# Last matrix product in seven products: row scaling on ScalarE, products without weight sums first, high and low splits ordered by when they are due

## The chip, the cores and the metric

One core of one Trainium2 chip runs the whole program. The metric is the device time of one execution in microseconds (us); smaller is better. The engines are named as in the profile: PE (TensorE matmuls; PEld its weight loads), DVE (VectorE), ACT (ScalarE), POOL (GpSimd) and SP (SyncE, which issues the transfers here).

## The reference, cut to what matters

```python
attn = softmax(mask(q @ k.T / 8)) @ v            # 2 x 12 heads, 448 x 64, causal
x    = attn as 896 x 768
g    = h * sigmoid(h),  h = x @ moe_w_in         # 768 -> 2048
x    = g @ moe_w_out                             # 2048 -> 768
h    = x @ moe2_w_in                             # 768 -> 1024
e    = exp(h - max(h));  sm = e / (sum(e) + 1e-9)
solu = h * sm
ln   = (solu - mean) / sqrt(var + 1e-6) * g_ln   # over the 1024 columns
out  = ln @ moe2_w_out                           # 1024 -> 768
```

The change concerns the last two products and what lies between: `moe2_w_in` (called GEMM3 here), the chain of softmax and normalization, and `moe2_w_out` (GEMM4, weights `w4`).

## The kernel before, in words

**Precision.** Every matrix product runs on operands split into a high and a low part, and each step of the inner dimension is three matmuls: high by high, high by low, low by high. The high part is a copy on ACT, the low part a subtraction on DVE or POOL. Names that end in `h` and `l` are these parts. Weights arrive as 64-bit floats in chunks of 128 rows by 384 columns; each chunk is put together by one ACT operation (L275) and three bit operations on DVE (L280, L296, L286).

**GEMM3 and the chain.** 896 rows are 7 tiles of 128, t = 0 to 6. `gemm3(t)` makes `h` of one tile in PSUM. `chain` then does for this tile: maximum (DVE L675), exp (ACT L676), reciprocal (DVE L678, L679), product with h (DVE L680), mean (L681), square (ACT L683, which writes over `h` in PSUM), centring (ACT L684), and the power -1/2 of the variance (DVE L685, POOL L686). The result of a tile is the row `e`; its factor `rstd` is applied at the output. Two PSUM places hold `h`, so a tile's GEMM3 waits for L683 of two tiles before.

**GEMM4's weights.** The 16 chunks of `w4` are named as quarters "11", "12", "21", "22" (half of the rows, half of the columns), four chunks of each, k = 0 to 3. `feed4` takes them in while GEMM3 runs: `scale4` multiplies a chunk by `g_ln` (POOL L588), `high4` and `low4` split quarters 11, 21 and 22 (ACT L593, DVE L599), and after the four chunks of one k `sums4` forms the sums t1 to t4 of quarters in place (POOL L606 to L609). An engine's work is issued in the order in which the code calls it.

**GEMM4's products.** Tile 0 is multiplied plainly (`alone(0)` and `alone(1)`). Tiles 1 to 6 go in three pairs, and a pair's 2 x 2 quarters are multiplied by seven products instead of eight (`pair4`): 11·11, 12·21 and s4·22 with quarters of the weights, and s2·t2, s3·t3, s1·t1 and 22·t4 with weight sums. s1 to s4 are sums of quarters of the pair's own operand. Each product is 12 matmuls of 384 columns into one PSUM bank; its result is scaled by `rstd` and added to others (ACT L795, L796, DVE L786) and stored. The operand's quarters are transposed on PE (`turned`, L702, four transposes to a quarter), the sums formed by `sums` (ACT L725 copies, DVE L695 adds), and `parts` splits each (high ACT L691, low DVE or POOL L692); `take` calls it. Low parts of s1 to s4 are POOL's. Transposed quarters lie in two PSUM buffers (`tp`), so a further quarter waits until an earlier one has been read.

**The order.** After GEMM3: the first quarters of pair 0, `split_t` of t2 (ACT L869, DVE L870), then `alone(0)`, `split_t` of t3, the chain of tile 6 with `split_t` of t1 and t4 called inside it, then the three pairs. Between a pair's products, `ahead(g)` turns, sums and splits the operand of the next pair, step n after the n-th product.

Of the kernel before, what the change touches and what calls it, by code (L numbers as in the profile page):

```python
# [26 lines left out]
K2 = KF2 // 2  # L27
# [53 lines left out]
def fused(ctx, tc, qk, vv, w1, w2, w3, w4, gl, out):  # L81
# [11 lines left out]
    wring = pool("wring", 4)  # L93

    ident = const.tile([128, 128], F32, name="ident")

    def pad(where, count):
        where.tile([128, count // 4], F32, name="pad", tag="pad", bufs=1)

    pad(act, 64)  # L100
    pad(gap, 192)
    xhl = act.tile([128, 2, KD, T], F32R, name="x", tag="a")
    xh, xl = xhl[:, 0], xhl[:, 1]
# [2 lines left out]
    with tc.manual_schedule():  # L106
# [361 lines left out]
        for f in range(KF):  # L468
            if f == 1:
                gps[f, 1] = gm.tile([128, 512], F32, name="ps", tag="gm")  # L470
            else:
                t = pair()
                for b in range(B):
                    if f >= 2 or b == 1:
                        gps[f, b] = t[b]
            for half in range(2):
                for b in range(B):
                    if f >= 2 or b == 1:
                        gemm1(f, half, b)
                m = 2 * f + half + 4  # L480
                feed_to(*((1, m) if m < N12 else (2, m - N12)))
            for b in range(B):
                if f >= 2 or b == 1:
                    silu(f, b)
        warm = const.tile([128, 1], F32, name="warm")
        nc.scalar.activation(warm, ident[:, :1], AF.Exp)
        sgr.release()
# [84 lines left out]
        aop = {z: [dp.tile([128, K2, 128], F32R, name=f"a{z}{q}", tag=f"a{z}{q}") for q in "hl"]  # L572
               for z in ("u1", "u2", "11")}
        usum = dp.tile([128, K2, 128], F32, name="us", tag="us")
        gain = dp.tile([128, KF2], F32, name="gain", tag="gain", bufs=1)
        nc.sync.dma_start(gain, gl)

        def quad(m):
            n, k = divmod(m, KF2)
# [4 lines left out]
        def scale4(m):  # L584
            z, k = quad(m)
            x = quads[z, k] = wx.pop((4, m))
            g = gain[:, m % KF2:m % KF2 + 1]
            nc.gpsimd.tensor_scalar(x, x, g, None, ALU.mult)  # L588

        def high4(m):  # L590
            z, k = quad(m)
# [16 lines left out]
            nc.gpsimd.tensor_tensor(b22, b22, b11, ALU.subtract)  # L608
            nc.gpsimd.tensor_tensor(b21, b21, b22, ALU.subtract)  # L609

        scaled = []

        def feed4():
            m = fed[0]
            fed[0] += 1
            while scaled:
                old = scaled.pop(0)
                high4(old)
                low4(old)
            for _ in range(2):  # L620
                if len(pend) > (_ > 0):
                    old = order[pend.pop(0)][1]
                    scale4(old)
                    scaled.append(old)
            if m < len(order):
                conv_b(*order[m], x4, order[m + 1] if m + 1 < len(order) else None)
                pend.append(m)
            if m + 1 < len(order):
                conv_a(*order[m + 1])
            if m + RAWS < len(order):  # L630
                load_w(*order[m + RAWS])

# [33 lines left out]
        def half(t, n):  # L666
            return row(t)[:, K2 * n:K2 * n + K2]

        def chain(t, fill, fill2):
            ps = hps[t]  # L670
            s = dp.tile([128, 12], F32, name="s", tag="s", bufs=NT)
            es4[t] = dp.tile([128, KF2, 128], F32, name="e", tag="e", bufs=NT - 1)
            e, p4 = row(t), ps.rearrange("p n (m q) -> p (n m) q", m=K2)
            col = lambda m: s[:, m:m + 1]
            nc.vector.tensor_reduce(col(0), ps, AX.XY, ALU.max, negate=True)  # L675
            nc.scalar.activation(e, p4, AF.Exp, bias=col(0), accum_out=col(1))  # L676
            fill()
            nc.vector.tensor_scalar(col(2), col(1), 1e-9, None, ALU.add)  # L678
            nc.vector.reciprocal(col(3), col(2))  # L679
            nc.vector.scalar_tensor_tensor(e, e, col(3), p4, ALU.mult, ALU.mult, accum_out=col(4))  # L680
            nc.vector.tensor_scalar(col(5), col(4), -1.0 / DF2, None, ALU.mult)  # L681
            fill2()
            nc.scalar.activation(p4, e, AF.Square, bias=col(5), accum_out=col(6))  # L683
            nc.scalar.activation(e, e, AF.Identity, bias=col(5))  # L684
            nc.vector.tensor_scalar(col(7), col(6), 1.0 / DF2, 1e-6, ALU.mult, ALU.add)  # L685
            nc.gpsimd.tensor_tensor(col(9), col(7), mhalf, ALU.pow)  # L686
            rstd[t] = col(9)

        def parts(z, x, low):
            h, l = aop[z]  # L690
# [90 lines left out]
        def pair4(g, between):  # L781
            a, b = 2 * g + 1, 2 * g + 2
            ra, rb = rstd[a], rstd[b]

            def scaled_sum(o, ps, r, more):
                nc.vector.scalar_tensor_tensor(o, ps, r, more, ALU.mult, ALU.add)  # L786

            def made(z, q):
                ps = bank()
                product(ps, z, q, True, True)  # L790
                return ps

            ps = made("11", "11")
            m1a, m1b = four()
            nc.scalar.activation(m1a, ps, AF.Copy, scale=ra)  # L795
            nc.scalar.activation(m1b, ps, AF.Copy, scale=rb)  # L796
            between(0)
            ps = made("s2", "t2")
            u2a, u2b = four()
            scaled_sum(u2a, ps, ra, m1a)  # L800
            scaled_sum(u2b, ps, rb, m1b)
            between(1)
            ps = made("12", "21")
            c11, c22 = four()
            scaled_sum(c11, ps, ra, m1a)
            store(a, 0, c11)
            between(2)
            ps = made("s3", "t3")
            u3, v = four()
            scaled_sum(u3, ps, rb, u2b)  # L810
            between(3)
            ps = made("s1", "t1")
            scaled_sum(c22, ps, rb, u3)
            store(b, 1, c22)
            scaled_sum(v, ps, ra, u2a)
            between(4)
            ps = made("22b" if g % 2 else "22", "t4")
            c21, c12 = four()
            scaled_sum(c21, ps, rb, u3)
            store(b, 0, c21)  # L820
            between(5)
            ps = made("s4", "22")
            scaled_sum(c12, ps, ra, v)
            store(a, 1, c12)
            between(6)

        def fill():
            if scaled or pend or fed[0] < len(order):
                feed4()

        for t in range(NT):
            gemm3(t, (lambda: turn(0, "11")) if t == NT - 1 else None)
            if t == 0:
                fill()
            if t == NT - 3:
                turn_alone()
            if t == NT - 2:
                turn(0, "21")
                turn(0, "22")

            def first():
                if t == NT - 3:
                    take_alone()
                if t == NT - 2:
                    sums(0, [1])
                fill()

            if t < NT - 1:
                chain(t, first, fill)
        while scaled or pend or fed[0] < len(order):  # L850
            fill()
        take(0, "11")
        sums(0, [2, 3])
        area = act.tile([128, 2 * KD * T], F32R, name="area", tag="a")[:, 8:]
        take(0, "s2")
        take(0, "22")
        turn(0, "12")
        take(0, "12")
# [2 lines left out]
        banks[1] = pool("psq", 2, space=PS)  # L861
        w3p.release()
        t4p = pool("t4", side="right")

        def split_t(z, q):
            split[4, z] = [t4p.tile([128, K2, CH], F32R, name=f"{z}{p}", tag=f"{z}{p}") for p in "hl"]
            h, l = split[4, z]
            for k in range(K2):
                nc.scalar.activation(h[:, k], quads[q, k], AF.Copy)  # L869
                nc.vector.tensor_tensor(l[:, k], quads[q, k], h[:, k].bitcast(F32), ALU.subtract)  # L870

        split_t("t2", "22")
        take(0, "s3")
        alone(0)
        split_t("t3", "12")
        take(0, "s1")
        take(0, "s4")

        def split_sum():
            take(0, "us")  # L880

        chain(NT - 1, lambda: split_t("t1", "11"), lambda: (split_t("t4", "21"), split_sum()))

        pad(t4p, 224)

        def ahead(g):
            def step(n):
                if g > 2:
                    return
                if n == 1:  # L890
                    turn(g, "21")
                    turn(g, "22")
                    sums(g, [1])
                    take(g, "22")
                if n == 2:
                    turn(g, "11")
                    take(g, "11")
                    sums(g, [2, 3])
                    take(g, "s2")
                if n == 3:  # L900
                    turn(g, "12")
                    take(g, "12")
                    sums(g, [4])
                    take(g, "s3")
                if n == 4:
                    take(g, "s1")
                if n == 6:
                    take(g, "s4")
            return step

        for g in range(3):
# [56 lines left out]
```

## Time and profile before

| | |
|---|---|
| median of 3 runs | 446.78 us (446.25 to 447.24) |
| profiled execution, own time | 446.85 us |
| its span in the trace | 445.1 us |
| mean granted TensorE clock | 0.979 |
| PE busy | 421.1 us (95%) |
| DVE busy | 351.2 us (79%) |
| POOL busy | 233.9 us (53%) |
| ACT busy | 230.6 us (52%) |
| chain that ended last, by engine | PE 80%, DVE 11%, ACT 4%, POOL 3% |

The span runs from the first to the last instruction of the trace; the profiled execution's own time is 1.75 us longer. GEMM3 ends and GEMM4 begins near 362 us; the last matmul starts near 440 us. Busy shares are means over stages with different limits, so the text below reads stretches, not means.

### The profile page before, as it was taken

What the parts mean: (1) busy time and instruction counts of PE and PEld (TensorE: products, weight loads), DVE (VectorE), ACT (ScalarE), POOL (GpSimd) and SP (SyncE); (2) the same over time, 40 slices, a digit from 0 to 9 for tenths busy, and PEclk for the clock granted to TensorE, in tenths of its full rate; (3) what the DMA queues carried; (4) which work ended last, traced back from release to release, by engine and by line L of the source; (5) the groups of instructions that cost most, each with busy time, mean ns of one, the idle gap of its engine ahead of it and who ended that gap; (6) DMA issues with size and microseconds to landing.
All of it is one profiled execution on the core that took longest, in us unless ns stands there. A gap on an engine that the chain in (4) does not pass through costs nothing.

```text
span 445.1 us, 7468 instructions
## 1 busy us (share of the span) xinstructions
PE 421.1 (95%) x2581; PEld 375.0 (84%) x2581; DVE 351.2 (79%) x744; ACT 230.6 (52%) x536; POOL 233.9 (53%) x245
## 2 busy tenths in 40 slices
PE   8999999999999999999999999999989975769995
PEld 6667777999999999999999999998868755769995
DVE  4999997999999989886958889577796877584631
ACT  5999997444343443444434444343663754752300
POOL 3996973676776757542534344244466277223300
PEclk9999999999999999999999999999999995969999
DMA  8941414243243333454747575241232100001112
GB/s 270 351 159 47 160 30 129 71 143 117 98 142 104 110 112 102 122 161 144 219 138 225 160 215 181 83 130 36 71 108 68 38 1 1 18 18 54 54 42 64
DMA packets 19798, 50.03 MB, mean 112 GB/s; under 512 B 2352, under 2 KB 4528, under 8 KB 19760
## 3 DMA queue, kind: packets, MB, share of 16 engines
q1 hardware_dynamic: 19760, 49.56, 35.3%
q8 instruction: 20, 0.33, 0.3%
q14 instruction: 18, 0.15, 0.1%
HBM read 46.80 MB, written 2.75 MB: 111 GB/s over the span
## 4 chain that ended last, share of the span: by engine, by line
PE 80%; DVE 11%; ACT 4%; POOL 3%; issue 1%; POOLq 0%; SPq 0%; ACTq 0%
PE h L371 8%; PE h L370 8%; PE h L372 8%; PE h L497 7%; PE h L496 7%; PE h L498 7%; PE x L248 5%; PE ps L756 4%; PE ps L758 4%; PE ps L757 4%; DVE e L188 3%; PE x L158 2%; PE x L222 2%; PE x L168 2%; ACT e L676 2%; DVE s L675 2%
## 5 line engine op out<-in xcount | busy, mean ns | idle before, releaser
L306 POOL TENSOR_TENSOR wl<-wx,wh 128x384 fp32r<-128x384 f32 x64 | 79.3, 1241 | 90.9 <-ACT wh L302 88.6
L286 DVE SCALAR_TENSOR_TENSOR wx<-wr,wx 128x384 uint32<-128x384 uint32 x96 | 69.9, 728 | 0.1
L275 ACT ACTIVATE wr<-wr 128x384 f32<-128x384 f32 x96 | 52.8, 555 | 32.7 <-DMA wr<-w_in 32.6
L302 ACT ACTIVATE wh<-wx 128x384 fp32r<-128x384 f32 x64 | 33.4, 522 | 65.5 <-DVE wx L286 33.6
L371 PE MATMUL h<-x,wh 128*128 128x448 f32 x174 | 63.2, 363 | 0.0
L370 PE MATMUL h<-x,wh 128*128 128x448 f32 x174 | 63.1, 362 | 0.0
L296 DVE TENSOR_SCALAR wr<-wr 128x384 uint32<-128x384 uint32 x96 | 60.4, 631 | 2.9 <-DMA wr<-w_in 2.8
L372 PE MATMUL h<-x,wl 128*128 128x448 f32 x174 | 62.6, 360 | 0.0
L280 DVE SCALAR_TENSOR_TENSOR wx<-wr 128x384 uint32<-128x384 uint32 x96 | 61.1, 636 | 1.3 <-POOL gl L380 1.3
L497 PE MATMUL h<-gl,wh 128*128 128x448 f32 x160 | 58.1, 363 | 0.0
L496 PE MATMUL h<-gh,wh 128*128 128x448 f32 x160 | 58.0, 362 | 0.0
L498 PE MATMUL h<-gh,wl 128*128 128x448 f32 x160 | 57.6, 360 | 0.0
L208 POOL TENSOR_TENSOR e<-e,st 128x384 f32<-128x384 f32 (+3 forms) x72 | 46.2, 677 | 14.1 <-ACT e L194 6.9
L380 POOL TENSOR_TENSOR gl<-sg,gh 128x448 fp32r<-128x448 f32 x32 | 41.0, 1281 | 15.3 <-DVE gh L379 14.6
L194 ACT ACTIVATE e<-e,st 128x128 f32<-128x128 f32 (+3 forms) x84 | 43.6, 523 | 4.3 <-DVE st L188 4.3
L188 DVE CUSTOM_DVE_ANT_0 e<-x,mask 128x384 f32<-128x384 f32 (+3 forms) x84 | 33.0, 443 | 4.7 <-PE x L158 4.7
L654 PE MATMUL h<-w3h,y 128*128 128x512 f32 x84 | 33.4, 397 | 2.0 <-ACT h L683 2.0
L370 PEld LDWEIGHTS h<-x,wh 128*128 128x128 f32 x174 | 32.7, 188 | 2.6
L372 PEld LDWEIGHTS h<-x,wl 128*128 128x128 f32 x174 | 32.5, 187 | 2.3
L371 PEld LDWEIGHTS h<-x,wh 128*128 128x128 f32 x174 | 32.7, 188 | 1.6
L656 PE MATMUL h<-w3h,y 128*128 128x512 f32 x84 | 32.9, 391 | 0.0
L655 PE MATMUL h<-w3l,y 128*128 128x512 f32 x84 | 32.8, 391 | 0.0
(184 smaller groups left out, 896.2 us busy)
## 6 DMA issues: line engine op xcount, KB each, us to landing
wr<-w_in SPq DMA_DIRECT2D x96, 384.0 KB, 3.6
qk<-qk_in SPq DMA_DIRECT2D x11, 480.0 KB, 5.3
v<-vv_in SPq DMA_DIRECT2D x12, 256.0 KB, 6.2
out<-o SPq DMA_DIRECT2D x12, 192.0 KB, 1.9
out<-ou SPq DMA_DIRECT2D x4, 96.0 KB, 2.2
qk<-qk_in SPq DMA_DIRECT2D x2, 128.0 KB, 2.3
qk<-qk_in SPq DMA_DIRECT2D x1, 224.0 KB, 2.6
gain<-gl_in SPq DMA_DIRECT2D x1, 4.0 KB, 1.5
```

What stands on the lines that cost most here:

```text
L188: nc.vector.tensor_tensor_reduce(o, scs[p, u[0], u[1]], m, -SCALE, 3.0e38, ALU.add, ALU.min, st[p % 4][:, COL[u]:COL[u] + 1])
L275: nc.scalar.activation(high, high, AF.Copy, scale=DOWN)
L280: nc.vector.scalar_tensor_tensor(x.bitcast(U32), r[:, :, 1], 0x80000000, r[:, :, 0], ALU.bitwise_and, ALU.bitwise_or)
L286: nc.vector.scalar_tensor_tensor(xu, r[:, :, 1], 3, xu, ALU.logical_shift_left, ALU.bitwise_or)
L296: nc.vector.tensor_scalar(low, low, 29, None, ALU.logical_shift_right)
L306: eng.tensor_tensor(l, wx.pop((n, c)), h.bitcast(F32), ALU.subtract)
L370: nc.tensor.matmul(ps[:, :S], wh, rh, start=turn == 0 and k % NB == 0, stop=False)
L371: nc.tensor.matmul(ps[:, :S], wh, rl, start=False, stop=False)
L372: nc.tensor.matmul(ps[:, :S], wl, rh, start=False, stop=turn == 1 and k % NB == NB - 1)
L496: nc.tensor.matmul(ps[:, :S], wh, rh, start=f == 0, stop=False)
L497: nc.tensor.matmul(ps[:, :S], wh, rl, start=False, stop=False)
L498: nc.tensor.matmul(ps[:, :S], wl, rh, start=False, stop=f == KF - 1)
```

## The change

1. `gain` (the vector `g_ln`) moves into a pool that lives from the start, and its transfer is issued earlier.
2. `scale4` becomes an ACT activation (copy with a scale per row) in place of POOL's `tensor_scalar`, 16 times.
3. `feed4` scales and splits off the high parts of up to two chunks at once, then puts together the next chunk, then calls `low4`, whose last act is `sums4`.
4. A pair's products come in the order 11·11, 12·21, s4·22, s2·t2, s3·t3, s1·t1, 22·t4; before it was 11·11, s2·t2, 12·21, s3·t3, s1·t1, 22·t4, s4·22. The output sums are regrouped to suit.
5. `chain` becomes a generator with three stops. The chain of tile 6 and `split_t` of t3, t1 and t4 move into pair 0, between its products (`begin`). t1's low parts go to POOL. The turning of the next pair comes one or two steps later.

```diff
+    gain = const.tile([128, KF2], F32, name="gain")
...
+        nc.sync.dma_start(gain, gl)
         warm = const.tile([128, 1], F32, name="warm")
...
-            g = gain[:, m % KF2:m % KF2 + 1]
-            nc.gpsimd.tensor_scalar(x, x, g, None, ALU.mult)
+            nc.scalar.activation(x, x, AF.Copy, scale=gain[:, m % KF2:m % KF2 + 1])
...
-            while scaled:
-                old = scaled.pop(0)
-                high4(old)
-                low4(old)
-            for _ in range(2):
-                if len(pend) > (_ > 0):
-                    old = order[pend.pop(0)][1]
-                    scale4(old)
-                    scaled.append(old)
+            old = [order[pend.pop(0)][1] for _ in range(min(2, len(pend) - (len(pend) > 2)))]
+            for c in old:
+                scale4(c)
+                high4(c)
             if m < len(order):
                 conv_b(*order[m], x4, order[m + 1] if m + 1 < len(order) else None)
                 pend.append(m)
             if m + 1 < len(order):
                 conv_a(*order[m + 1])
+            for c in old:
+                low4(c)
...
-            ps = made("s2", "t2")
-            u2a, u2b = four()
-            scaled_sum(u2a, ps, ra, m1a)
-            scaled_sum(u2b, ps, rb, m1b)
-            between(1)
             ps = made("12", "21")
             c11, c22 = four()
             scaled_sum(c11, ps, ra, m1a)
             store(a, 0, c11)
+            between(1)
+            ps = made("s4", "22")
+            m13, u3 = four()
+            scaled_sum(m13, ps, ra, m1a)
             between(2)
+            ps = made("s2", "t2")
+            u2a, u2b = four()
+            scaled_sum(u2a, ps, ra, m13)
+            scaled_sum(u2b, ps, rb, m1b)
+            between(3)
             ps = made("s3", "t3")
...
+        def split_t(z, low=None):
+            q = {"t1": "11", "t2": "22", "t3": "12", "t4": "21"}[z]
             h, l = split[4, z]
             for k in range(K2):
                 nc.scalar.activation(h[:, k], quads[q, k], AF.Copy)
+                (low or nc.vector).tensor_tensor(l[:, k], quads[q, k], h[:, k].bitcast(F32), ALU.subtract)
...
+        late = chain(NT - 1)
+        next(late)
+
+        def begin(n):
+            if n == 0:
+                split_t("t3")
+                take(0, "s3")
+            if n == 1:
+                next(late)
+                take(0, "s1")
+                split_t("t1", nc.gpsimd)
+            if n == 2:
+                split_t("t4")
+            if n == 3:
+                next(late)
+                take(0, "us")
 
         def ahead(g):
             def step(n):
+                if g == 1:
+                    begin(n)
                 if g > 2:
                     return
-                if n == 1:
+                if n == 2:
                     turn(g, "21")
                     turn(g, "22")
                     sums(g, [1])
                     take(g, "22")
-                if n == 2:
+                if n == 3:
                     turn(g, "11")
                     take(g, "11")
                     sums(g, [2, 3])
-                    take(g, "s2")
-                if n == 3:
+                if n == 4:
                     turn(g, "12")
                     take(g, "12")
                     sums(g, [4])
+                    take(g, "s4")
+                if n == 5:
+                    take(g, "s2")
                     take(g, "s3")
-                if n == 4:
+                if n == 6:
                     take(g, "s1")
```

How this changes the order on the engines, at the three places that matter below. Line numbers of the changed kernel differ a little: L587 is the scaling, L592 and L598 the high and low parts of the quarters, L677 and L678 the square and the centring, L686, L687 and L690 the operand's high parts, low parts and adds, L867 and L868 the high and low parts of the t's, L669, L672 to L675 and L679 the chain on DVE, L680 the power on POOL, L781 the scaled sums.

ACT at the end of GEMM3, before. `b11h`, `b21h`, `b22h` are high parts of quarters, `a11h` the high part of pair 0's first operand quarter:

```order
L593 ACTIVATE b22h<-wx 128x384
L275 ACTIVATE wr<-wr 128x384
L593 ACTIVATE b11h<-wx 128x384
L683 ACTIVATE h,s<-e,s 128x1024
L684 ACTIVATE e<-e,s 128x1024
L593 ACTIVATE b21h<-wx 128x384
L593 ACTIVATE b22h<-wx 128x384
L691 ACTIVATE a11h<-tp 128x512
```

The same place after:

```order
L587 ACTIVATE wx<-wx,gain 128x384
L276 ACTIVATE wr<-wr 128x384
L587 ACTIVATE wx<-wx,gain 128x384
L592 ACTIVATE b21h<-wx 128x384
L677 ACTIVATE h,s<-e,s 128x1024
L678 ACTIVATE e<-e,s 128x1024
L587 ACTIVATE wx<-wx,gain 128x384
L592 ACTIVATE b22h<-wx 128x384
L686 ACTIVATE a11h<-tp 128x512
```

Each chunk's scaling now stands on ACT just ahead of its high part, and one chunk fewer is left behind the centring.

DVE at the same place, before (the add at the top belongs to pair 0's operand sums; the rows from L678 are the chain of tile 5):

```order
L695 TENSOR_TENSOR e<-tp,e 128x512
L599 TENSOR_TENSOR b22l<-wx,b22h 128x384
L280 SCALAR_TENSOR_TENSOR wx<-wr 128x384
L296 TENSOR_SCALAR wr<-wr 128x384
L286 SCALAR_TENSOR_TENSOR wx<-wr,wx 128x384
L678 TENSOR_SCALAR s<-s 128x1
L679 RECIPROCAL s<-s 128x1
L680 SCALAR_TENSOR_TENSOR e,s<-e,s,h 128x1024
L681 TENSOR_SCALAR s<-s 128x1
```

The same place after:

```order
L690 TENSOR_TENSOR e<-tp,e 128x512
L281 SCALAR_TENSOR_TENSOR wx<-wr 128x384
L297 TENSOR_SCALAR wr<-wr 128x384
L287 SCALAR_TENSOR_TENSOR wx<-wr,wx 128x384
L672 TENSOR_SCALAR s<-s 128x1
L673 RECIPROCAL s<-s 128x1
L674 SCALAR_TENSOR_TENSOR e,s<-e,s,h 128x1024
L675 TENSOR_SCALAR s<-s 128x1
```

The low part of quarter 22, whose end starts the weight sums on POOL, no longer stands there; it has been done earlier, and the weight sums of that k with it.

DVE in pair 0, from the last add before the splits of the t's, before (`t2l`, `t3l`, `t1l`, `t4l` are low parts; L675 to L681 the chain of tile 6):

```order
L695 TENSOR_TENSOR e<-tp,e 128x512
L870 TENSOR_TENSOR t2l<-wx,t2h 128x384 x4
L870 TENSOR_TENSOR t3l<-wx,t3h 128x384 x4
L675 TENSOR_REDUCE s<-h 128x1
L870 TENSOR_TENSOR t1l<-wx,t1h 128x384 x4
L678 TENSOR_SCALAR s<-s 128x1
L679 RECIPROCAL s<-s 128x1
L680 SCALAR_TENSOR_TENSOR e,s<-e,s,h 128x1024
L681 TENSOR_SCALAR s<-s 128x1
L870 TENSOR_TENSOR t4l<-wx,t4h 128x384 x4
L685 TENSOR_SCALAR s<-s 128x1
L786 SCALAR_TENSOR_TENSOR o<-ps,s,o 128x384 x2
```

The same place after:

```order
L868 TENSOR_TENSOR t2l<-wx,t2h 128x384 x4
L669 TENSOR_REDUCE s<-h 128x1
L868 TENSOR_TENSOR t3l<-wx,t3h 128x384 x4
L781 SCALAR_TENSOR_TENSOR o<-ps,s,o 128x384
L672 TENSOR_SCALAR s<-s 128x1
L673 RECIPROCAL s<-s 128x1
L674 SCALAR_TENSOR_TENSOR e,s<-e,s,h 128x1024
L675 TENSOR_SCALAR s<-s 128x1
L781 SCALAR_TENSOR_TENSOR o<-ps,s,o 128x384
L868 TENSOR_TENSOR t4l<-wx,t4h 128x384 x4
L690 TENSOR_TENSOR e<-tp,e 128x512
L687 TENSOR_TENSOR area<-tp,area 128x512
```

t1's low parts are gone from DVE, t4's stand ahead of the add of pair 1's first sum (L690), and the outputs of pair 0 come earlier. POOL in the same stretch, after (`area` rows are low parts of s4, s2, s3 and s1):

```order
L605 TENSOR_TENSOR wx<-wx 128x384
L606 TENSOR_TENSOR wx<-wx 128x384
L607 TENSOR_TENSOR wx<-wx 128x384
L608 TENSOR_TENSOR wx<-wx 128x384
L687 TENSOR_TENSOR area<-e,area 128x512 x4
L868 TENSOR_TENSOR t1l<-wx,t1h 128x384 x4
L680 TENSOR_TENSOR s<-s,mhalf 128x1
L687 TENSOR_TENSOR area<-us,area 128x512
```

Before, the `area` row of x4 was followed by that of `us` and the power; the four low parts of t1 are new on POOL between them.

## Rows read from the trace of the kernel before

**Rows 1.** Waits of PE from 300 us on: total us, times, longest us.

```profile
PE tp L702 <- DVE e L695: 8.1, 1, 8.1
PE tp L702 <- ACT e L725: 6.4, 1, 6.4
PE h L654 <- ACT h L683: 2.0, 2, 1.4
```

**Rows 2.** Timeline of PE: the restarts behind the two long waits, and the last matmuls.

```profile
372.37 1.08 PE L702 MATMUL tp<-ident,e 128*128 128x128 f32 x4 [8.15 <-DVE e L695]
...
393.52 1.11 PE L702 MATMUL tp<-ident,e 128*128 128x128 f32 x4 [6.38 <-ACT e L725]
...
440.04 0.33 PE L757 MATMUL ps<-t3l,au1h 128*128 128x384 f32 x1
440.21 0.34 PE L758 MATMUL ps<-t3h,au1l 128*128 128x384 f32 x1
```

**Rows 3.** Timeline of ACT around the first long wait: start, us, operation, [idle before <- releaser].

```profile
363.71 0.53 ACT L593 ACTIVATE b11h<-wx 128x384 fp32r<-128x384 f32 x1 [4.33 <-POOL wx L588]
364.38 1.12 ACT L683 ACTIVATE h<-e,s 128x1024 f32<-128x1024 f32 x1
365.65 1.15 ACT L684 ACTIVATE e<-e,s 128x1024 f32<-128x1024 f32 x1
369.10 0.52 ACT L593 ACTIVATE b22h<-wx 128x384 fp32r<-128x384 f32 x1 [0.70 <-POOL wx L588]
369.52 0.58 ACT L691 ACTIVATE a11h<-tp 128x512 fp32r<-128x512 f32 x1
```

**Rows 4.** Timeline of DVE: shifts and low parts beside POOL, and the first two undisturbed.

```profile
326.94 0.35 DVE L296 TENSOR_SCALAR wr<-wr 128x384 uint32<-128x384 uint32 x1
327.21 0.55 DVE L286 SCALAR_TENSOR_TENSOR wx<-wr,wx 128x384 uint32<-128x384 uint32 x1
...
360.10 1.18 DVE L296 TENSOR_SCALAR wr<-wr 128x384 uint32<-128x384 uint32 x1
361.19 1.37 DVE L286 SCALAR_TENSOR_TENSOR wx<-wr,wx 128x384 uint32<-128x384 uint32 x1
...
369.65 0.78 DVE L599 TENSOR_TENSOR b22l<-wx,b22h 128x384 fp32r<-128x384 f32 x1 [0.66 <-ACT b22h L593]
...
370.96 1.27 DVE L695 TENSOR_TENSOR e<-e,tp 128x512 f32<-128x512 f32 x2
```

**Rows 5.** Timeline of POOL beside the stretched shifts of rows 4.

```profile
359.86 1.20 POOL L608 TENSOR_TENSOR wx<-wx 128x384 f32<-128x384 f32 x1 [1.47 <-DVE b22l L599]
```

**Rows 6.** Groups by shape: busy us, mean ns | idle before, releaser.

```profile
L206 ACT ACTIVATE e<-e,st 128x384 f32<-128x384 f32 x3 | 1.9, 635 | 0.0
L588 POOL TENSOR_SCALAR wx<-wx,gain 128x384 f32<-128x384 f32 x16 | 21.1, 1334 | 2.2 <-DMA gain<-gl_in 2.2
```

**Rows 7.** Windows: range, length, busy of PE (xN), PEld, DVE, ACT, POOL; PEclk, DMA.

```profile
373.46:378.30 4.84, 4.84 (x16) 4.84 (x16) 4.28 (x7) 2.76 (x6) 2.84 (x2) 0.50 0.00 0
392.10:398.92 6.82, 5.40 (x20) 5.31 (x21) 5.50 (x11) 3.08 (x6) 1.33 (x2) 0.50 0.08 29
```

**Rows 8.** A piece of the chain that ended last: one matmul's place, us.

```profile
394.63 0.32 PE ps L756
```

**Rows 9.** Timelines of ACT and DVE in pair 0.

```profile
375.33 3.04 DVE L870 TENSOR_TENSOR t2l<-wx,t2h 128x384 fp32r<-128x384 f32 x4
...
380.51 1.76 ACT L869 ACTIVATE t3h<-wx 128x384 fp32r<-128x384 f32 x4
382.17 1.14 ACT L691 ACTIVATE area<-e 128x512 fp32r<-128x512 f32 x2
...
385.84 1.97 DVE L870 TENSOR_TENSOR t1l<-wx,t1h 128x384 fp32r<-128x384 f32 x4 [1.69 <-ACT t1h L869]
```

**Rows 10.** Timelines: low parts of `w3` on DVE and POOL at the same time.

```profile
304.16 2.43 DVE L306 TENSOR_TENSOR w3l<-wx,w3h 128x384 fp32r<-128x384 f32 x2 [0.16 <-ACT w3h L302]
...
305.04 1.14 POOL L306 TENSOR_TENSOR w3l<-wx,w3h 128x384 fp32r<-128x384 f32 x1 [0.16 <-ACT w3h L302]
```

More of the change, by code (lines that the diff above doesn't have):

```diff
@@ L95, in fused @@
     ident = const.tile([128, 128], F32, name="ident")
+    gain = const.tile([128, KF2], F32, name="gain")
     def pad(where, count):
         where.tile([128, count // 4], F32, name="pad", tag="pad", bufs=1)
-    pad(act, 64)
+    pad(act, 32)
     pad(gap, 192)
@@ L574, in fused @@
         usum = dp.tile([128, K2, 128], F32, name="us", tag="us")
-        gain = dp.tile([128, KF2], F32, name="gain", tag="gain", bufs=1)
-        nc.sync.dma_start(gain, gl)
         def quad(m):
@@ L609, in sums4 @@
             nc.gpsimd.tensor_tensor(b21, b21, b22, ALU.subtract)
-        scaled = []
         def feed4():
@@ L667, in half, with chain @@
             return row(t)[:, K2 * n:K2 * n + K2]
-        def chain(t, fill, fill2):
+        def chain(t):
             ps = hps[t]
@@ L676, in chain @@
             nc.scalar.activation(e, p4, AF.Exp, bias=col(0), accum_out=col(1))
-            fill()
+            yield
             nc.vector.tensor_scalar(col(2), col(1), 1e-9, None, ALU.add)
@@ L681, in chain @@
             nc.vector.tensor_scalar(col(5), col(4), -1.0 / DF2, None, ALU.mult)
-            fill2()
+            yield
             nc.scalar.activation(p4, e, AF.Square, bias=col(5), accum_out=col(6))
@@ L687, in chain @@
             rstd[t] = col(9)
+            yield
         def parts(z, x, low):
@@ L806, in pair4 @@
             store(a, 0, c11)
+            between(1)
+            ps = made("s4", "22")
+            m13, u3 = four()
+            scaled_sum(m13, ps, ra, m1a)
             between(2)
+            ps = made("s2", "t2")
[3 more added lines that the diff above has]
+            between(3)
             ps = made("s3", "t3")
-            u3, v = four()
             scaled_sum(u3, ps, rb, u2b)
-            between(3)
+            between(4)
             ps = made("s1", "t1")
+            c21, c12 = four()
             scaled_sum(c22, ps, rb, u3)
             store(b, 1, c22)
-            scaled_sum(v, ps, ra, u2a)
-            between(4)
+            scaled_sum(c12, ps, ra, u2a)
+            store(a, 1, c12)
+            between(5)
             ps = made("22b" if g % 2 else "22", "t4")
-            c21, c12 = four()
             scaled_sum(c21, ps, rb, u3)
             store(b, 0, c21)
[L821 to L824, printed above, removed]
             between(6)
         def fill():
-            if scaled or pend or fed[0] < len(order):
+            if pend or fed[0] < len(order):
                 feed4()
@@ L848, in fused @@
             if t < NT - 1:
-                chain(t, first, fill)
-        while scaled or pend or fed[0] < len(order):
+                for more in zip(chain(t), (first, fill, lambda: None)):
+                    more[1]()
+        while pend or fed[0] < len(order):
             fill()
@@ L854, in fused @@
         area = act.tile([128, 2 * KD * T], F32R, name="area", tag="a")[:, 8:]
-        take(0, "s2")
         take(0, "22")
@@ L863, in fused @@
         t4p = pool("t4", side="right")
-        def split_t(z, q):
+        for z in ("t2", "t3", "t1", "t4"):
             split[4, z] = [t4p.tile([128, K2, CH], F32R, name=f"{z}{p}", tag=f"{z}{p}") for p in "hl"]
+        pad(t4p, 224)
+        def split_t(z, low=None):
+            q = {"t1": "11", "t2": "22", "t3": "12", "t4": "21"}[z]
             h, l = split[4, z]
@@ L869, in split_t @@
                 nc.scalar.activation(h[:, k], quads[q, k], AF.Copy)
-                nc.vector.tensor_tensor(l[:, k], quads[q, k], h[:, k].bitcast(F32), ALU.subtract)
-        split_t("t2", "22")
-        take(0, "s3")
+                (low or nc.vector).tensor_tensor(l[:, k], quads[q, k], h[:, k].bitcast(F32), ALU.subtract)
+        take(0, "s4")
+        split_t("t2")
+        take(0, "s2")
         alone(0)
[L875 to L884, printed above, removed]
+        late = chain(NT - 1)
[13 more added lines that the diff above has]
+                take(0, "us")
         def ahead(g):
             def step(n):
+                if g == 1:
+                    begin(n)
                 if g > 2:
                     return
-                if n == 1:
+                if n == 2:
                     turn(g, "21")
@@ L903, in step @@
                     sums(g, [4])
+                    take(g, "s4")
+                if n == 5:
+                    take(g, "s2")
                     take(g, "s3")
-                if n == 4:
+                if n == 6:
                     take(g, "s1")
-                if n == 6:
-                    take(g, "s4")
             return step
```

## The prediction, made before the changed kernel ran

> **What bounds the kernel now.** I read the page first. PE is busy 95% of the span, so time can be won only where PE stands, or where it runs at a lower clock. I then asked for PE's waits in the part that the change touches. Two long ones stand there, 8.1 and 6.4 us, and two short ones in GEMM3 of 2.0 together, the longer 1.4, the shorter so 0.6 [rows 1]. The timeline puts the long ones at 364.2 to 372.37 and 387.1 to 393.52 [rows 2].
>
> *First wait.* PE wants to turn a second quarter of pair 0 and needs a `tp` buffer free. The last to read it is DVE's add, behind DVE's low part of `a11`, behind ACT's high part `a11h` at 369.52, and that stands on ACT behind `b22h`, which waited for POOL's scaling [rows 3]. So POOL's scaling of the last weight chunks is what PE waits for in the end. Ahead of it ACT stood 4.33 for an earlier chunk, with the square L683 queued behind it until 364.38. DVE was late too: two shifts took 1.18 and 1.37 at 360.1 and 361.2, where undisturbed they take 0.35 and 0.55 [rows 4]; POOL ran the weight sum L608 beside them [rows 5] and L609 after it.
>
> *Second wait.* The add's partner is an ACT copy, L725. ACT runs in order, and ahead of the copy stand the high parts of t1 and t4, the square and the centring of tile 6, and pair 0's first two outputs. Nothing that PE needs next depends on tile 6's chain; it is only ahead in the queue.
>
> *The clock.* After both long waits the granted clock is 0.50, the 1.2 GHz level, until PE has been busy a while [rows 7]; matmuls then come 0.32 apart [rows 8] where at the full level they come 0.17 apart, 0.173 over longer stretches [rows 2]. The first such stretch, 16 matmuls, loses 16 x 0.147 = 2.4; I take the second, 12 matmuls and 8 transposes, as 2.4 too.
>
> **Step A, GEMM3.** 16 POOL scalings, 21.1 us [rows 6], go. ACT gets 16 scalings by row of 128x384. The trace has no such ACT operation on these tiles; the nearest row, a scaled ACT operation of the same shape, takes 0.635 [rows 6]. That is 10.2 us on ACT, which is half idle here. The page's 2.0 us of short waits [rows 1] come from L683 standing late behind waits for POOL; bounds are 0 and -2.0, and I take -0.8, because the scalings that replace the waits stand on the same queue. Moving the `gain` transfer earlier costs nothing: it lies beside GEMM2.
>
> **Step B, first wait.** The square of tile 5 starts at 364.38 before. It comes earlier by 0.8 (A), by 0.83 + 0.82 = 1.65 since the two shifts of rows 4 no longer have a weight sum beside them, and by 0.47 since `b22l` no longer stands ahead on DVE: 361.5. Centring starts 1.27 later (364.38 to 365.65 [rows 3]), 362.75, and ends at 363.9. Then the last scaling, 0.6, and `b22h`, 0.42 (369.10 to 369.52 [rows 3]): `a11h` starts at 364.95 instead of 369.52. From there to PE's restart it was 372.37 - 369.52 = 2.85; I add 0.4, since `b22l` (0.78 before [rows 4]) now runs beside a POOL weight sum and comes to about 1.2. **PE restarts at 368.2, 4.2 earlier**, after a wait of 368.2 - (364.2 - 0.8) = 4.8.
>
> **Step C, the list to the next stand.** From the restart PE has 72 matmuls ahead (alone(0) 24, then 11·11, 12·21, s4·22, s2·t2) and 12 transposes: 72 x 0.173 + 1.4 = 13.9, so 382.1, or 384.5 with 2.4 of low clock. The next stand is the copy of pair 1's first quarter on ACT. t2's low parts ended 6.0 after the restart before (378.37 [rows 9] against 372.37); s4's high part, 0.57, now stands ahead and one more low part meets POOL's (+0.8): 368.2 + 7.4 = 375.6. Behind it: maximum and exp of tile 6, 1.2 each by L683's passes of the same size [rows 3], 378.0; two outputs of 11·11 at 0.57, 379.1; t3's high parts 1.66 (380.51 to 382.17 [rows 9]); two area copies 1.14 [rows 9]; t1's and t4's high parts 1.66 each; the copy, 0.6: **385.8**. ACT sets this, so the clock matters little: PE stands 1.3 or 3.7 here.
>
> **Step D, t1 and t4 side by side.** t1's low parts go to POOL and t4's run on DVE at the same time, from 384.2. On DVE alone four low parts take 1.97 [rows 9]. Where DVE and POOL made low parts at the same time, two on DVE took 2.43 [rows 10], 1.2 each, and POOL's 1.14. So I price four pairs at 1.25: 389.2. Behind them in DVE's queue stands the add that PE needs, then ACT's high part and DVE's low part of that quarter, three operations near 0.635 (half of 1.27 [rows 4]): 391.1. PE has a turn (0.5) and s3·t3 (12 x 0.173 = 2.1) from 385.8, 388.4, and stands 2.8 until **391.2**. What it bounds: none of the collision, t4l done by 386.1; each waiting out the other's whole operation, 1.14 + 1.2 = 2.35 a pair, 4.4 more. I take the row's 1.25.
>
> The Trainium skill (SBUF — State Buffer, section SBUF: two separate sides) calls the shared pair of VectorE and GpSimd "an exclusive lock, not a bandwidth split": whichever starts first holds it for the whole instruction. It speaks against giving t1 to GpSimd at all; [rows 4, 5] agree for the shifts (0.35 becomes 1.18). By it a pair would cost POOL's operation plus DVE's, about 1.6, and the time 1.4 more.
>
> **Step E, the rest.** Before, from the restart at 393.52 to the end of the last matmul, 440.21 + 0.34 = 440.55 [rows 2], it was 47.03. After, two products (s3·t3 and one more) and a turn already lie behind at 391.2: 24 x 0.173 + 0.45 = 4.6. And the low clock of the second restart, 2.4, goes, if a stand of 2.8 is like the short ones (1.4 [rows 1], after which the page's clock stays at 9 tenths) and not like the 6.4. 391.2 + 47.0 - 4.6 - 2.4 = 431.2.
>
> **The sum.** The profiled execution took 446.85, 6.3 behind the last matmul; 431.2 + 6.3 = 437.5. Pairs 1 and 2 run in the new order too, and their waits are not priced: between nothing and the longer short wait, 1.4; I take the shorter, 0.6 [rows 1]. **438.1**, or -8.7 against 446.85, which is the median of the runs, 446.78, within 0.1.
>
> A check by place: PE stands 2.0 + 8.15 + 6.4 = 16.5 before, and 1.2 (A) + 4.8 (B) + 1.3 (C, with the low clock ahead of it) + 2.8 (D) + 0.6 after, 10.7. The 5.8 between them and the 2.4 of one low clock less make 8.2, the sum within half a us.
>
> **The rivals.**
>
> *1. No collision.* POOL and DVE might work on t1 and t4 without holding each other up; then t4l ends at 386.1, the operand at 388.0, before PE is there: 2.8 less, 435.3. Against it stand rows 4, 5 and 10; for it, that copies on ACT pace both engines at 0.42 a piece, so that they needn't fall together each time.
>
> *2. A heavier collision, or the low clock again.* By the bound of step D, 4.4 more; by the summed operations, 1.4; and with the low clock after the last stand, 2.4 more: 439.5 to 442.5. For it: the clock did fall at both waits of over 6 us, and step B leaves 4.8 in one and step D close to 3.
>
> *3. ScalarE becomes the bound of GEMM3: slower.* If the 16 scalings all lay on the path, 16 x 0.635 = 10.2 would be added to 438.1: 448.3. It decides from 8.7 / 16 = 0.54 us a scaling on the path. For: PE already waits for ACT's L683 twice [rows 1], and the scalings stand on ACT's queue between exp and square. Against: ACT stood 4.33 idle just ahead of the last square [rows 3] and is busy 52% of the span; it would need to be late for nearly all tiles.
>
> *4. The first wait stays*, because the chain of tile 5 is still ahead of the last chunk on ACT; the change then doesn't bring POOL's late work forward, and step B's 4.2 is lost, and as ACT paces step C all of it comes through: 442.3.
>
> **Chances.** The forecast, with 437 to 439.5 as its own range, 0.52; rival 1, 0.12; rival 2, 0.20; rival 3, 0.10, of which 0.04 falls between, where part of the scalings is on the path; rival 4, 0.06. The range from 434.5 (rival 1 with all of step A's 2.0) to 443.0 (rival 2's upper end) leaves out rival 3 and the tails. 0.2% is 0.9 us, about what a measurement of this kernel can tell from no change. Faster by over that 0.90, within it 0.04, slower 0.06.
>
> **What would show it.** A: no wait of ACT for POOL in GEMM3, and PE's waits on the square shorter. B: `a11h` near 365 and PE's restart near 368. C: PE waits for ACT's copy near 386. D: t1l on POOL and t4l on DVE stretched to about 1.25 each, and PE waiting for DVE near 391. E: granted clock above 0.9 after 392. The prediction is wrong if PE waits on GEMM3's chains for more than 2.3 in all, if t4l isn't stretched, or if a wait appears in pair 1 or 2.

## The result, and the profile after

The changed kernel takes 440.56 us (median of 4 runs, 439.22 to 441.31) against 446.69 before on the same chip: a ratio of 0.9859, 95% interval 0.9831 to 0.9886, 6.1 us less. On a second chip (experiment e5) it was 0.9862 (0.9844 to 0.9879). The forecast was 438.1, with 437 to 439.5 as its own range and 434.5 to 443.0 as the whole one. The profiled execution took 440.92, its span is 439.1; the numbers below are from it.

PE's waits after the start, from the view of waits of the changed kernel (to be laid beside [rows 1]):

```profile
PE tp L697 <- DVE e L690: 5.0, 1, 5.0
PE tp L697 <- DVE area L687: 2.8, 1, 2.8
PE tp L697 <- ACT e L720: 2.0, 1, 2.0
...
PE h L648 <- ACT h L677: 1.3, 2, 0.7
PE x L159 <- DMA qk<-qk_in: 1.2, 1, 1.2
```

The 8.1 became 5.0, the 6.4 became 2.0 and 2.8, GEMM3's 2.0 became 1.3: the stands that the forecast named. The wait of 1.2 for a load at the very start is not among the waits of the kernel before. The timeline of PE shows where the stands end, when GEMM3 begins, and the last matmul (compare [rows 2]):

```profile
302.74 0.40 PE L648 MATMUL h<-w3h,y 128*128 128x512 f32 x1
...
369.65 1.09 PE L697 MATMUL tp<-ident,e 128*128 128x128 f32 x4 [5.04 <-DVE e L690]
...
387.51 0.66 PE L697 MATMUL tp<-ident,e 128*128 128x128 f32 x4 [2.04 <-ACT e L720]
...
393.12 0.63 PE L697 MATMUL tp<-ident,e 128*128 128x128 f32 x4 [2.83 <-DVE area L687]
...
434.25 0.34 PE L753 MATMUL ps<-t3h,au1l 128*128 128x384 f32 x1
```

In the trace of before, GEMM3 began at 301.28:

```profile
301.28 0.40 PE L654 MATMUL h<-w3h,y 128*128 128x512 f32 x1
```

So everything here stands 1.46 later from a cause ahead of the changed stage. Taken off, the restarts are at 368.2, 386.05 and 391.65, and the last matmul ends at 433.1.

The timelines of ACT and DVE at the first wait (compare [rows 3, 4]):

```profile
363.07 1.12 ACT L677 ACTIVATE h<-e,s 128x1024 f32<-128x1024 f32 x1 [0.60 <-DVE s L675]
...
366.46 0.58 ACT L686 ACTIVATE a11h<-tp 128x512 fp32r<-128x512 f32 x1
...
360.44 0.36 DVE L297 TENSOR_SCALAR wr<-wr 128x384 uint32<-128x384 uint32 x1
360.71 0.55 DVE L287 SCALAR_TENSOR_TENSOR wx<-wr,wx 128x384 uint32<-128x384 uint32 x1
```

The two shifts are back at 0.36 and 0.55, since no weight sum runs beside them. The scaling's own price, from the groups by shape (compare [rows 6]):

```profile
L587 ACT ACTIVATE wx<-wx,gain 128x384 f32<-128x384 f32 x16 | 9.7, 607 | 2.3 <-DVE wx L287 2.3
```

What it still waits for is DVE, which puts the chunk together. The stretch behind the last stand, from the view of windows (compare [rows 7]):

```profile
392.90:398.90 6.00, 5.78 (x26) 5.81 (x27) 4.49 (x10) 3.12 (x6) 1.84 (x2) 0.72 0.01 3
```

A mean granted clock of 0.72 says that part of these 6 us ran at the 1.2 GHz level. The forecast had 0.9 or more there.

And the two engines side by side, from the timelines of DVE and POOL (compare [rows 9, 10]):

```profile
386.13 4.88 DVE L868 TENSOR_TENSOR t4l<-wx,t4h 128x384 fp32r<-128x384 f32 x4
...
385.75 4.86 POOL L868 TENSOR_TENSOR t1l<-wx,t1h 128x384 fp32r<-128x384 f32 x4
```

Four low parts take 4.88 on DVE beside four on POOL, 1.22 a pair.

### The profile page after: what moved, and what is told of

It reads as the page before. It is cut to its first block, busy times and chain, and to the rows that moved or that the text cites. A ratio compares the mean times of both kernels' runs of the same rounds, so it can differ in the third digit from the quotient of the medians.

```text
span 439.1 us, 7462 instructions
## 1 busy us (share of the span) xinstructions
PE 418.8 (95%) x2581; PEld 372.6 (85%) x2581; DVE 350.4 (80%) x740; ACT 239.3 (55%) x552; POOL 218.5 (50%) x233
## 4 chain that ended last, share of the span: by engine, by line
PE 82%; DVE 11%; ACT 4%; DMA 1%; issue 1%; SPq 0%; ACTq 0%
PE h L372 8%; PE h L371 8%; PE h L373 8%; PE h L499 7%; PE h L498 7%; PE h L500 7%; PE x L249 5%; PE ps L751 3%; PE ps L753 3%; PE ps L752 3%; PE x L223 3%; PE h L648 3%; PE h L649 3%; PE x L159 3%; PE h L650 2%; DVE e L189 2%
## 5 line engine op out<-in xcount | busy, mean ns | idle before, releaser
L307 POOL TENSOR_TENSOR wl<-wx,wh 128x384 fp32r<-128x384 f32 x64 | 80.3, 1256 | 89.9 <-ACT wh L303 87.5
L287 DVE SCALAR_TENSOR_TENSOR wx<-wr,wx 128x384 uint32<-128x384 uint32 x96 | 67.6, 704 | 0.1
L297 DVE TENSOR_SCALAR wr<-wr 128x384 uint32<-128x384 uint32 x96 | 58.6, 612 | 3.3 <-DMA wr<-w_in 3.1
```

Source lines behind the costliest of these rows:

```text
L287: nc.vector.scalar_tensor_tensor(xu, r[:, :, 1], 3, xu, ALU.logical_shift_left, ALU.bitwise_or)
L297: nc.vector.tensor_scalar(low, low, 29, None, ALU.logical_shift_right)
L307: eng.tensor_tensor(l, wx.pop((n, c)), h.bitcast(F32), ALU.subtract)
```

## The experiments

Each ran in a group of four on one chip, beside before on that chip. "From GEMM3's start" below takes the start of each trace off, so that what happens at the beginning of an execution doesn't count. GEMM3's length runs from its first matmul to the beginning of PE's first long stand (301.28 to 364.22 in the trace of before, 302.74 to 364.61 in that of the changed kernel). Gains of single experiments are worked out from the ratio to before on the same chip, unless a text gives two times.

**e1: the scaling on ScalarE alone, in the kernel before.**

```diff
-            g = gain[:, m % KF2:m % KF2 + 1]
-            nc.gpsimd.tensor_scalar(x, x, g, None, ALU.mult)
+            nc.scalar.activation(x, x, AF.Copy, scale=gain[:, m % KF2:m % KF2 + 1])
```

> Before, with the 16 row scalings on ScalarE and nothing else changed. Queue theory (the first long wait is ACT's queue behind POOL's scaling, and what is won there comes through because ACT paces the next stretch): the short waits of PE in GEMM3 fall from 2.0 to about 1.2, the square of tile 5 stays near 363.6 (its predecessors on DVE are still stretched by a weight sum), a11h comes near 367.5 instead of 369.5, PE's first restart near 370.3, the second wait stays as long as it was; time about 444.0. Rival (the scaling is hidden, the gain of the change is all in the order of the products): 446.7. Rival (ScalarE becomes the bound of GEMM3): over 448.

Measured: ratio 0.9999 (0.9978 to 1.0020), no change. The expected 444.0 was missed, and neither rival's reason fits either: the wait for POOL is gone, and the restart still comes only 0.7 earlier (70.4 from GEMM3's start against 71.1). The timelines of DVE and ACT show why:

```profile
360.17 1.18 DVE L296 TENSOR_SCALAR wr<-wr 128x384 uint32<-128x384 uint32 x1
361.27 1.37 DVE L286 SCALAR_TENSOR_TENSOR wx<-wr,wx 128x384 uint32<-128x384 uint32 x1
...
364.45 1.12 ACT L682 ACTIVATE h<-e,s 128x1024 f32<-128x1024 f32 x1 [3.57 <-DVE s L680]
365.72 1.15 ACT L683 ACTIVATE e<-e,s 128x1024 f32<-128x1024 f32 x1
366.78 0.60 ACT L587 ACTIVATE wx<-wx,gain 128x384 f32<-128x384 f32 x1
367.41 0.52 ACT L592 ACTIVATE b21h<-wx 128x384 fp32r<-128x384 f32 x1
367.84 0.60 ACT L587 ACTIVATE wx<-wx,gain 128x384 f32<-128x384 f32 x1
368.47 0.52 ACT L592 ACTIVATE b22h<-wx 128x384 fp32r<-128x384 f32 x1
368.90 0.58 ACT L690 ACTIVATE a11h<-tp 128x512 fp32r<-128x512 f32 x1
```

ACT now waits 3.57 for DVE instead of 4.33 for POOL. The two shifts ahead of the square on DVE are still stretched by the weight sums, which accounts for some 1.6 of it. And behind the centring two scalings and two high parts, 2.1 us, stand ahead of `a11h`. The old feed order puts both there. The trace of e1 is 2.9 shorter than that of before from GEMM3's start to the end of the last matmul (136.4 against 139.3), though the medians are the same: the restart makes 0.7 of it, and most of the rest is that PE's lower clock behind the first stand lasted a shorter time in this execution (see the last section).

**e2: the changed kernel with the scaling back on GpSimd.**

```diff
-            nc.scalar.activation(x, x, AF.Copy, scale=gain[:, m % KF2:m % KF2 + 1])
+            nc.gpsimd.tensor_scalar(x, x, gain[:, m % KF2:m % KF2 + 1], None, ALU.mult)
```

> The changed kernel with the scaling back on GpSimd and all else kept. Queue theory: POOL's scaling is the releaser of the last high parts again, a11h near 369 to 370, PE's first restart 2 to 4 us later than 369.65, and as ACT paces the rest most of it stays: 442.5 to 444.5. Rival (the new order of products and splits absorbs a late first restart): within 1 us of 440.6.

Measured: 447.42, ratio to before 1.0028 (1.0010 to 1.0046), so worse than expected and worse than before. The restart at 376.42 is late by more than the expected 2 to 4, and most of that lies ahead of the first wait, which is even shorter, 3.2. The view of PE's waits:

```profile
PE h L648 <- ACT h L677: 7.7, 3, 3.4
PE tp L697 <- DVE e L690: 3.2, 1, 3.2
```

And a line of ACT's timeline:

```profile
360.79 0.52 ACT L592 ACTIVATE b11h<-wx 128x384 fp32r<-128x384 f32 x1 [5.54 <-POOL wx L587]
```

In the new feed order a high part stands on ACT directly where its scaling is issued. With the scaling on POOL, ACT stands 5.54 in front of `b11h` with the square queued behind, and GEMM3 waits for the square: 71.2 us long instead of 61.9. PE's waits make 6.4 of these 9.3 us (7.7 against 1.3); behind its two longest stands in GEMM3, 3.35 and 2.88, the granted clock fell as well, to 0.52 and 0.53 over the next 3 us.

**e6: scaling on ScalarE and the new feed order in the kernel before, old order of products.** The edit is e1's and the `feed4` of the change.

> Before, with ScalarE's row scalings and the new feed order (scaling and high parts at once, low parts and weight sums after the next chunk), but the old order of the products and of the t splits. Theory (scaling and feed order together make the first restart earlier, neither does alone): GEMM3 62.0 long from its start, a11h 63.8 after GEMM3's start instead of 68.2, PE's first restart 67.0 after it instead of 71.1, the second wait still near 6.4, and the time 4 us below before, 441.8. Rival (what is won at the first wait is given back at the second): within 1 us of before.

Measured: 442.03, ratio 0.9924 (0.9903 to 0.9945), 3.4 less than before, where 4 was expected. GEMM3 is 62.1 long, `a11h` comes 63.9 and the restart 67.1 after its start, and the second wait is 6.4: each as expected, and nothing is given back. Lines of PE and ACT:

```profile
368.73 0.82 PE L696 MATMUL tp<-ident,e 128*128 128x128 f32 x4 [5.01 <-DVE e L689]
388.66 1.12 PE L696 MATMUL tp<-ident,e 128*128 128x128 f32 x4 [6.41 <-ACT e L719]
...
375.16 0.58 ACT L768 ACTIVATE ou<-ps,s 128x384 f32<-128x384 f32 x1 [2.81 <-PE ps L752]
```

The second stand is as long here as in before and e1 (6.41, 6.38 and 6.38), though PE restarts earlier: in the old order of products ACT's list ahead of the copy begins with an output that waits for PE, so it moves along with PE.

**e7: the new order of products and splits alone**, with scaling and feed order of before. Points 4 and 5 of the change are tested together here, not apart.

> The changed kernel with scaling on GpSimd and the feed order of before; the new order of products and of the t splits is kept. Theory: the first restart 71.1 after GEMM3's start as before; the second wait of 6.4 is replaced by two of 2 to 3; 3 us below before, 442.8. Rival (the new order only pays when the first restart is early): within 1 us of before.

Measured: 444.08, ratio 0.9957 (0.9943 to 0.9971), 1.9 less than before. PE's waits are 8.2 (8.15 before), then 2.0 and 2.9; the restart is 71.1 after GEMM3's start. The gain is smaller than the 3 expected. Lines of PE, and the window behind the last stand:

```profile
390.71 0.66 PE L702 MATMUL tp<-ident,e 128*128 128x128 f32 x4 [1.98 <-ACT e L725]
396.32 0.63 PE L702 MATMUL tp<-ident,e 128*128 128x128 f32 x4 [2.86 <-DVE area L692]
...
396.30:402.30 6.00, 5.98 (x27) 5.98 (x28) 4.49 (x9) 2.92 (x6) 1.85 (x2) 0.72 0.01 3
```

The stands themselves are only 1.5 shorter (1.98 and 2.86 against 6.38), and the lower clock comes back behind the second. The two halves give 3.4 and 1.9, together 5.3, and the whole change 6.1 (5.4 to 7.0 by e5's interval): they add up as well as these measurements can tell.

**e5: the changed kernel once more.** No edit.

> The changed kernel once more, unaltered, beside the others on one chip. In its first trace GEMM3 began at 302.74, 1.46 later than before, out of a wait for the first loads. Theory (that delay belongs to the execution): GEMM3 begins near 301.6, as in the variants with the same beginning (301.6 and 301.8), the way from there to the last matmul is 131.9 again with PE's waits 5.0, 2.0 and 2.8 and a lower clock behind the last, and the time is 439.5 to 440.5. Rival (the earlier transfer of gain or the other addresses delay the start): GEMM3 begins at 302.7 again.

Measured: 439.81, ratio 0.9862. GEMM3 begins at 302.00, and from there to the end of the last matmul it is 131.8, as in the first trace (131.85). The granted clock fell again behind the last stand:

```profile
392.30:398.50 6.20, 6.14 (x28) 6.17 (x29) 4.69 (x10) 2.96 (x6) 1.83 (x2) 0.72 0.01 3
```

GEMM3 began at 300.9 to 302.0 in every trace but the first of the changed kernel (302.74), with the early transfer of `gain` or without, so that delay belonged to the execution and not to the kernel, as far as one trace of each can tell.

**e3: t1's low parts on VectorE.**

```diff
-                split_t("t1", nc.gpsimd)
+                split_t("t1")
```

> The changed kernel with t1's low parts on VectorE as before, none on GpSimd. Collision theory (t1l on POOL and t4l on DVE hold each other up, 4.9 us for four pairs): t1l takes 1.97 from 385.7, t4l another 1.97 behind it, the add that PE waits for starts near 390.2 instead of 390.94, PE restarts near 392.3 instead of 393.12; time 0.8 less, about 439.8. Rival (the two engines share the work and the stretched times are not lost): the add comes later by the 2 us of t1l, 442.5.

Measured: 437.25, ratio 0.9807 (0.9783 to 0.9832); 2.4 less than the changed kernel by the ratios to before on each chip (3.3 less than its 440.56 and 2.6 less than e5's 439.81, each on another chip). The timelines of DVE and PE:

```profile
384.65 2.01 DVE L868 TENSOR_TENSOR t1l<-wx,t1h 128x384 fp32r<-128x384 f32 x4
387.11 1.95 DVE L868 TENSOR_TENSOR t4l<-wx,t4h 128x384 fp32r<-128x384 f32 x4
...
391.16 0.63 PE L697 MATMUL tp<-ident,e 128*128 128x128 f32 x4 [1.84 <-DVE area L687]
```

And the window behind that stand:

```profile
391.00:397.00 6.00, 5.84 (x35) 5.87 (x36) 4.49 (x10) 3.06 (x6) 1.84 (x2) 1.00 0.02 4
```

All eight low parts on one engine, 2.01 and 1.95, take less than four on each of two, 4.88. The restart is 1.0 earlier from GEMM3's start, near the expected 0.8. The rest, some 1.6 from the restart to the end of the last matmul (39.9 against 41.5), I had not expected: the stand fell from 2.8 to 1.84, and behind it the granted clock stayed at 1.00.

**e4: in each step the turning first, then the splits of t's.**

```diff
             def step(n):
-                if g == 1:
-                    begin(n)
...
                 if n == 6:
                     take(g, "s1")
+                if g == 1:
+                    begin(n)
```

> The changed kernel, but in each step between pair 0's products the turning for pair 1 is issued ahead of that step's splits of t's, so that t4's high and low parts stand behind the copy and the add that PE waits for. Queue theory: ACT's copy comes 1.7 earlier (no t4h ahead of it), the add 4 earlier (no t4l ahead of it); PE's waits of 2.0 and 2.8 shrink to under 1.5 together, what is left being t1's low parts on POOL; no wait of over 1.5 is left behind 375 us, the granted clock stays at the upper level after 385 (1.6 us), and the time is about 435.7, between 434.8 and 437. Rival (PE then waits for t4l or t1l itself as long as it did for the add): 439 to 440.6.

Measured: 434.27, ratio 0.9740 (0.9715 to 0.9765), below the expected 435.7, and half a us below its range. PE's waits:

```profile
PE tp L697 <- DVE e L690: 5.0, 1, 5.0
...
PE tp L697 <- ACT e L720: 0.4, 1, 0.4
PE ps L753 <- POOL area L687: 0.3, 1, 0.3
```

The two later stands are all but gone, and the granted clock is 1.00 from 385 to 430, though t1's low parts are still on POOL and still meet t4's: POOL 4.27, DVE 3.28. The copy comes 1.7 earlier from GEMM3's start than in the changed kernel, as expected, and the add 4.8. The product 22·t4 comes last in the pair, so t4 can be late. The edit also puts tile 6's square and centring behind the turning of its step.

**e8: e4, and the square of tile 5 and the last scaling behind `a11h`.**

```diff
-            if t < NT - 1:
+            if t < NT - 2:
                 for more in zip(chain(t), (first, fill, lambda: None)):
                     more[1]()
-        while pend or fed[0] < len(order):
-            fill()
+            if t == NT - 2:
+                rest = chain(t)
+                next(rest)
+                first()
+                next(rest)
+                fill()
         take(0, "11")
         sums(0, [2, 3])
+        while pend or fed[0] < len(order):
+            fill()
+        next(rest)
```

> The kernel with t4's splits behind the turning, and besides the square and centring of tile 5 and the last scaling stand behind a11h on ScalarE, and the low part of 22 behind the two adds on VectorE. Queue theory: a11h about 2.5 earlier, PE's first restart about 3 earlier, the wait there 2.0 instead of 5.0 and no lower clock behind it (1.5); as ACT had 7 us idle in the stretch that follows, 2 to 3.5 us come through: 431.5, between 430.5 and 432.5. Rival (the second PSUM bank, which waits for the square, or the weight sums of the last k, which come later, take the place of the wait): 434.

Measured: 432.17, ratio 0.9699 (0.9677 to 0.9722), 13.4 less than before and the fastest here. The timelines of ACT and PE:

```profile
361.41 0.58 ACT L686 ACTIVATE a11h<-tp 128x512 fp32r<-128x512 f32 x1
...
365.54 0.63 PE L697 MATMUL tp<-ident,e 128*128 128x128 f32 x4 [2.68 <-DVE e L690]
```

And the window behind that stand:

```profile
365.50:371.00 5.50, 5.46 (x24) 5.49 (x25) 3.15 (x6) 4.03 (x8) 3.73 (x4) 0.69 0.02 4
```

From GEMM3's start `a11h` is 3.3 and the restart 2.3 earlier than in e4, and 1.8 reaches the end of the last matmul. The lower clock behind a stand of 2.68 remains, against expectation.

## Why the prediction was right, and where it was off

**A and B held.** GEMM3's waits fell to 1.3, the longest 0.7 (forecast 1.2 in all), and the scaling no longer waits for POOL. Rival 3 is out, and so is rival 4. With the start's 1.46 taken off, the square stands at 361.6 (361.5 forecast), `a11h` at 365.0 (364.95), the restart at 368.2 (368.2), after 5.0 (4.8). A scaling took 0.607 (0.635). What the forecast did not say, and e1, e2 and e6 show, is that this step is of two edits that are worth nothing or less apart: scaling on ScalarE alone 0, both together 3.4, and the new feed order with POOL's scaling a loss of 3.2 by the ratios to before (e2 against e7, which differ in the feed order alone, on two chips).

**C held.** Restart at 386.05 without the start's shift (385.8), from ACT's copy, after 2.0. That ACT sets it and the clock doesn't matter is borne out: the restart lies 84.77 after GEMM3's start in the changed kernel's two traces and in e3's, though the lower clock behind the first stand lasted until 3.8, 4.1 and 5.7 us after the first restart. e4 shows what stood ahead of the copy: with t4's high parts behind it the stand is 0.4.

**D held.** 4.88 for four pairs, 1.22 each (1.25 forecast from [rows 10]); restart at 391.65 (391.2), 0.45 late. Rival 1, no collision, is out: t4's low parts took 4.88 beside t1's on POOL, and 1.95 without them (e3). The heavier collision of rival 2 is out too: 1.22 a pair is less than 1.6, POOL's operation added to DVE's at the forecast's prices. The Trainium skill's exclusive lock (SBUF — State Buffer, section SBUF: two separate sides) was read in that way in the forecast; the trace agrees with it that the two engines hold each other up, and differs from this reading on how much (1.22 against 1.6).

**E failed in one term: the low clock after the last stand.** The forecast took 2.4 off for it because a stand of 2.8 seemed like the short ones. The clock fell again, to a mean of 0.72 over 6 us. From the last restart to the end of the last matmul it was 434.59 - 393.12 = 41.47, where 40.0 were forecast: 1.5 more, ten matmuls at 0.147. That is the second half of rival 2, without its first half. e3 shows it from the other side: behind a stand of 1.84 no clock is lost, and the stretch takes 39.9. So the medians 440.56 and 439.81 lie outside the forecast's own range and in that of rival 2, 439.5 to 442.5, to which it gave 0.20.

**The start was not in the sum.** It is 1.46 of this execution. And the 0.6 set aside for waits in pairs 1 and 2 was not needed: none is in the list. That it made up for part of the clock's 1.5 is luck.

The terms: 438.1 + 1.46 (start) + 0.45 (D) + 1.47 (clock) - 0.6 = 440.9, and the profiled execution took 440.92. Without the start's delay it would be 439.5. e5's profiled execution, whose GEMM3 begins 0.72 later than that of before, took 440.15, and 439.5 + 0.72 = 440.2.

Open in part: why e7 brings 1.9 and not 3. Its trace is 3.25 shorter than that of before from GEMM3's start to the end of the last matmul, but behind first stands of 8.16 and 8.15 the lower clock lasted 3.8 us in e7 and 6.0 in before, seven matmuls fewer at 0.147, or 1.0. That belongs to these two executions; without it 2.2 is left, within the interval of 1.3 to 2.5. As before's own times on these two chips spread over 2 to 3.5 us, one trace each can't settle it.

## What to carry to other kernels

An edit that changes an engine and one that changes the order can be worth nothing apart and several us together: the scaling gave 0 (e1), the feed order lost 3.2 (e2 against e7), the two won 3.4 (e6). Ask for each what stands behind the instruction in its queue. When work is moved between products, issue first what the next turn of PE waits for, then what is due last; that was worth 5.4 us here (e4 against the changed kernel, by the ratios), while splitting the same work over two engines, which collided, lost 2.4 against one (e3), the lower clock behind the longer stand included.

## What the runs showed of the hardware

Eight low parts on DVE alone took 3.96 (2.01 and 1.95); four on DVE and four on POOL at the same time 4.88. The second engine made the work slower, in the traces of e3 and of the changed kernel.

The granted clock fell behind every stand of PE of 2.68 (e8) and longer in the last two products, and in e2 behind stands of 2.88 and 3.35 in GEMM3. It was still 1.00 behind stands of 1.84 (e3), 1.87 (e5), 1.98 (e7), 2.04 (the changed kernel) and 2.41 (e2); behind the last four the next stand, of 2.8 or 2.9, came 2.7 us after the restart, so these rows don't show what would have followed.

How long the lower stretch lasts differs from execution to execution, and not with the length of the stand alone. Behind first stands of 8.15 (before), 8.16 (e7) and 7.62 (e1) the matmuls came back to 0.17 apart after 6.0, 3.8 and 3.1 us. Behind first stands of 5.0 it was 3.8 and 4.1 in the changed kernel's two traces, 3.8 in e4, 3.5 in e6 and 5.7 in e3. The forecast's 2.4 for such a stretch was read from the longest of them; differences of 1 us between two single traces can come from this alone.
